# Attention with queries six tokens to a row, means in 32-column tiles, and scores on eight tiles at once

## The chip, the cores and the metric

The kernel runs on one core of a Trainium2 chip. The metric is the device time of the whole program in microseconds. One core has no second die to be compared with, so ratios are taken within one chip and one set of rounds; traces are also laid side by side across two chips (`e10` to `e13` ran on another chip than `e1` to `e9`). A span, from the first to the last instruction, is shorter than the time of the same run, in the runs below by 1.7 to 3.4 us.

In the lines of the profile PE is TensorE, DVE VectorE, ACT ScalarE, POOL GpSimd and SP SyncE. The results of PE lie in PSUM until VectorE or ScalarE copies them out; the kernel hands out PSUM's banks under the names `at`, `pk` and `pv`. A tiling says how PE's array is divided among small matmuls: `128*64` is two tiles of 128 rows by 64 columns. A filler is a matmul of zeros that only keeps PE busy.

## The reference

```python
a = exp(phi - max); a = a / sum(a)              # 8 batches, 8 heads, 576 tokens, 32 slots
k_m = einsum('bhsm,bhsd->bhmd', a, k)           # means of k and v over the tokens, d = 64
v_m = einsum('bhsm,bhsd->bhmd', a, v)
attn = softmax(q @ k_m.T / sqrt(64))            # 576 x 32 for each head
x = (attn @ v_m) ... reshape to (8, 576, 512)
x_prev = x shifted by one token
xk = mu_k * x + (1 - mu_k) * x_prev;  xr = mu_r * x + (1 - mu_r) * x_prev
out = sigmoid(xr @ w_r) * (relu(xk @ w_k)**2 @ w_v)      # 512 -> 1024 -> 512
```

The attention is small in arithmetic; the three products with the weights are large. The kernel interleaves both: the channel mix goes through the 4608 tokens in nine chunks of 512 with 16 groups of matmuls each (`pk` keys, `pr` gates, `pv` values), and the steps of one batch's attention stand between these groups at places that a table names.

## The kernel before

Tokens lie four to a row in 128 rows, with the last 64 of 576 as a fifth piece of 64 rows. The means of two heads are computed at once in 64 columns, the half of it that belongs to the other head being masked away afterwards:

```python
for j in range(NJ):                                   # NJ = 5 pieces of tokens
    for c in range(2):
        for jj in range(2):
            pr = 2 * c + jj
            nc.tensor.matmul(kvps[jj * 64:(jj + 1) * 64, c], lhsT=heads(j, pr * 64, 64),
                             rhs=kv5[:, parts, 2 * pr:2 * pr + 2, j, :], ...)
...
def tr_q(pr):                                          # queries: one head, one piece, 64 columns
    for j in range(NJ):
        for i in range(2):
            nc.tensor.matmul(ps[i * D:(i + 1) * D, j * 128:(j + 1) * 128],
                             lhsT=q5[:, 2 * pr + i, j, :], rhs=identity, is_transpose=True, ...)
...
def scores(c, hf):                                     # two tiles, one bank
    for jj in range(2):
        nc.tensor.matmul(ps[jj * 64:(jj + 1) * 64, :], lhsT=st["kmT"][:, c, jj, :],
                         rhs=st["qT"][:, 2 * c + jj, sl], ...)
...
def load_mu():                                         # mu, needed for the first two batches' mixing
    ... nc.vector.tensor_scalar_add(mu1, ps_mu, -1.0)
    for w in range(2):                                 # mu_b was loaded from ScalarE's queue at the start
        nc.vector.tensor_mul(mu_m[:, w, 0], mask, mu_b[:, w])
        nc.vector.tensor_sub(mu_m[:, w, 1], mask, mu_m[:, w, 0])
```

The softmax here doesn't subtract the row's maximum and nothing guards it: scores larger than these inputs give would overflow.

Of the kernel before, what the change touches and what calls it, by code (L numbers as in the profile page):

```python
# [17 lines left out]
STEADY = [("q2", -15), ("q0+pv", -15), ("q3+pk", -15), ("q1", -15), ("exp", -15), ("kv+pv", -14), ("z+pv",  # L18
          -14), ("nk", -13), ("nv", -13), ("load", -11), ("tk", -11), ("s3", -9), ("s1+pk", -9),
          ("s2", -8), ("s0+pv", -8), ("l0+pk", -6), ("l3", -6), ("l2", -5), ("l1+pk", -5), ("r0z",  # L20
          -4), ("r1z", -3), ("w0", -3), ("x0", 1), ("x1+pv", 2), ("w1", 2), ("x2", 7), ("x3", 8),
          ("dd", 9), ("k2d", 11), ("k0d", 13), ("r0d", 15), ("r2d", 23)]
FIRST = {
    0: [("exp", -58), ("busy23_232748", -54), ("mu", -48), ("k+pv", -47), ("z+pv", -45), ("busy1_400335",
        -45), ("q0", -43), ("nk", -41), ("busy1_690297", -41), ("q1", -39), ("tk", -39), ("s1+pv",
        -39), ("s0+pk", -38), ("q2", -37), ("busy2_979210", -37), ("l0", -36), ("q3", -32),
        ("l1+pk", -30), ("s3", -28), ("s2+pv", -26), ("r0z", -25), ("busy3_103560", -23), ("w0",
        -21), ("l2+pv", -20), ("l3+pv", -18), ("r1z", -18), ("v+pv", -15), ("busy1_899602", -15),
        ("nkx", -14), ("w1", -13), ("busy1_551200", -11), ("mk1", -11), ("mk0+pk", -11), ("mk2",
        -10), ("mk3+pv", -10), ("nrx", -5), ("load", -3), ("mr2+pv", 2), ("mr0+pk", 2), ("mr1", 2),  # L30
        ("mr3", 7)],
    1: [("exp", 5), ("k+pk", 8), ("z+pk", 8), ("nk", 9), ("tk+pk", 10), ("q3", 10), ("q2+pk", 10),
        ("q1+pv", 10), ("q0", 11), ("s0", 11), ("s2", 11), ("s3", 11), ("s1+pk", 12), ("l0", 12),
        ("l2+pv", 12), ("l1+pk", 12), ("r0z", 13), ("l3", 13), ("v", 13), ("w0", 13), ("nkx", 13),
        ("nrx", 13), ("r1z", 13), ("mk0", 13), ("w1", 13), ("mk1+pv", 13), ("mr3+pk", 14), ("mr1",
        14), ("mk3+pv", 14), ("mk2", 15), ("mr0+pv", 15), ("load", 16), ("mr2+pv", 17)],
    2: [("q3", -2), ("q0", -2), ("q1+pv", -2), ("exp", -2), ("kv", -1), ("q2", -1), ("z", -1), ("nk", -1),
        ("nv", -1), ("tk", 0), ("s2+pv", 1), ("s0", 1), ("s1", 1), ("s3", 1), ("l1", 3), ("l2+pv",
        3), ("l3", 4), ("l0", 4), ("r0z", 5), ("w0", 5), ("r1z", 5), ("x1+pv", 7), ("x0", 7), ("w1",
        7), ("load+pv", 8), ("x2", 8), ("x3+pk", 8), ("dd", 9), ("k0d", 12), ("r2d", 12), ("k2d",  # L40
        13), ("r0d", 13)],
    3: [("q0", -11), ("q2", -8), ("exp", -8), ("q1", -8), ("q3", -7), ("kv+pv", -7), ("z", -7), ("nk", -7),
        ("nv", -7), ("load+pv", -7), ("tk", -6), ("s2", -5), ("s3+pv", -5), ("s1", -5), ("s0", -5),
        ("l2+pv", -4), ("l3", -4), ("r1z", -4), ("w1", -4), ("l1", -4), ("l0+pk", -4), ("r0z", -4),
        ("w0", -2), ("x3", -1), ("x2", 1), ("x1", 7), ("x0", 8), ("dd", 8), ("k0d", 8), ("k2d", 11),
        ("r2d", 12), ("r0d", 15)],
}
ORDER = ('phi', 'k', 'q', 'wv', 'v')



NB = 4
TAIL = 512
# [3 lines left out]
def kernel(  # L57
# [24 lines left out]
    HALF = S // 2  # L82
    CT = 512
# [12 lines left out]
    qs = [const.tile([128, H, NJ, D], BF16, name=f"q{i}") for i in range(2)]  # L96
# [26 lines left out]

    def load_batch(b):
        load_phi(b, nc.gpsimd)
        load_rows(kvs[b % 2][:, 0], k[b])
        load_rows(qs[b % 2], q[b])
        load_rows(kvs[b % 2][:, 1], v[b])
# [3 lines left out]
    load_rows(qs[0], q[0], 2)  # L132
# [3 lines left out]
    for i in range(2):  # L136
        nc.vector.memset(kvs[i][64:128, :, :, NB, :].rearrange("p a h d -> p (a h) d"), 0.0)
        nc.vector.memset(ems[i][64:128, NB], 0.0)
        nc.vector.memset(qs[i][64:128, :, NB, :], 0.0)
# [5 lines left out]
    for w, mu in enumerate((moe_mu_k, moe_mu_r)):  # L145
        for jj in range(2):
            nc.scalar.dma_start(
                out=mu_b[jj * 64:(jj + 1) * 64, w],
                in_=mu.rearrange("(c j x) -> j c x", c=2, j=2)[jj:jj + 1].to_broadcast([64, 2, 2 * D]))
# [11 lines left out]
    for what in ORDER:  # L161
        if what == "wv":
            nc.gpsimd.dma_start(out=wv_sb, in_=wv_v)
        elif what == "phi":
            load_phi(1, nc.gpsimd)
        else:
            load_rows(qs[1] if what == "q" else kvs[1][:, "kv".index(what)], {"q": q, "k": k, "v": v}[what][1])
# [29 lines left out]

    def load_mu():
        ps_mu = psum.tile([128, 2 * ND], F32, name="psmu", tag="at", bufs=3)
        nc.tensor.transpose(ps_mu, mu2, ident_f)  # L200
        nc.vector.tensor_scalar_add(mu1, ps_mu, -1.0)

        for w in range(2):
            mask = maskk.rearrange("p h d -> p (h d)").unsqueeze(1).to_broadcast([128, 2, 2 * D])
            nc.vector.tensor_mul(mu_m[:, w, 0], mask, mu_b[:, w])
            nc.vector.tensor_sub(mu_m[:, w, 1], mask, mu_m[:, w, 0])


    def attention(b):
        st = {}  # L210

        def ps_tile(shape, dtype, name):

            tag = st.get("tag", "at")
            return psum.tile(shape, dtype, name=name, tag=tag, bufs={"at": 3, "pk": 2, "pv": 3}[tag])
        x0 = b * S % RING
        kv5, q5, em = kvs[b % 2], qs[b % 2], ems[b % 2]
# [9 lines left out]
        def ekv(parts):  # L227

            def go():
                w = parts.stop - parts.start  # L230
                kvps = ps_tile([128, 2, w, 2 * D], F32, "kvps")
                for i in range(w):
                    st["kv"[parts.start + i]] = kvps[:, :, i, :]
                for j in range(NJ):
                    for c in range(2):
                        for jj in range(2):
                            pr = 2 * c + jj
                            nc.tensor.matmul(kvps[jj * 64:(jj + 1) * 64, c], lhsT=heads(j, pr * 64, 64),  # L238
                                             rhs=kv5[:, parts, 2 * pr:2 * pr + 2, j, :],
                                             start=j == 0 and c == 0, stop=j == NB,  # L240
                                             skip_group_check=True)
# [11 lines left out]
        def norm_k():  # L253
            kbd = work.tile([128, 2, 2, D], BF16, name="kbd", tag="kbd")
            for c in range(2):
                nc.vector.scalar_tensor_tensor(
                    kbd[:, c].rearrange("p h d -> p (h d)"), in0=st["k"][:, c, :],
                    scalar=st["rz"][:, c:c + 1], in1=maskk.rearrange("p h d -> p (h d)"),
                    op0=AL.mult, op1=AL.mult)
            st["kbd"] = kbd  # L260

        def norm_v():
            vbd = work.tile([128, 2, 2, D], BF16, name="vbd", tag="vbd")
            for c in range(2):
                nc.vector.scalar_tensor_tensor(
                    vbd[:, c].rearrange("p h d -> p (h d)"), in0=st["v"][:, c],
                    scalar=st["rz"][:, c:c + 1], in1=maskk.rearrange("p h d -> p (h d)"),
                    op0=AL.mult, op1=AL.mult)
# [6 lines left out]
        def tr_k():  # L275
            ps = ps_tile([128, 2, 2, 64], BF16, "ktps")
            for c in range(2):
                nc.tensor.matmul(ps[:, c].rearrange("p j m -> p (j m)"),
                                 lhsT=st["kbd"][:, c].rearrange("p h d -> p (h d)"), rhs=identity,
                                 is_transpose=True, start=True, stop=True, skip_group_check=True)  # L280
            st["kmT"] = work.tile([128, 2, 2, 64], BF16, name="kmT", tag="kmT")
            nc.vector.tensor_copy(st["kmT"].rearrange("p c j m -> p (c j m)"),
                                  ps.rearrange("p c j m -> p (c j m)"))

        def tr_q(pr):
            def go():
                if "qT" not in st:
                    st["qT"] = work.tile([128, NPAIR, S], BF16, name="qT", tag="qT")
                ps = ps_tile([128, NJ * 128], BF16, "qtps")
                for j in range(NJ):  # L290
                    for i in range(2):
                        nc.tensor.matmul(ps[i * D:(i + 1) * D, j * 128:(j + 1) * 128],  # L292
                                         lhsT=q5[:, 2 * pr + i, j, :], rhs=identity,
                                         is_transpose=True, start=True, stop=True,
                                         skip_group_check=True)
                nc.vector.tensor_copy(st["qT"][:, pr, :], ps[:, 0:S])  # L296
            return go

        def scores(c, hf):
            def go():  # L300
                if "e" not in st:
                    st["e"] = work.tile([128, 2, S], BF16, name="e", tag="e")
                ps = ps_tile([128, HALF], F32, "scps")
                sl = slice(hf * HALF, (hf + 1) * HALF)
                for jj in range(2):
                    nc.tensor.matmul(ps[jj * 64:(jj + 1) * 64, :], lhsT=st["kmT"][:, c, jj, :],  # L306
                                     rhs=st["qT"][:, 2 * c + jj, sl], start=True, stop=True,
                                     skip_group_check=True)
# [256 lines left out]
```

## Time and profile before

| | before |
|---|---|
| time, median of 3 (range) | 233.19 us (232.72 to 234.55) |
| span of the profiled run | 231.6 us |
| first wide matmul (`pk`) | 23.25 us |
| from there to the start of PE's last instruction | 202.8 us |
| PE after that instruction's start to the end | 5.6 us |
| length of a chunk in the steady state | 22.7 us |

The span falls into a start, in which PE waits for loads and for a chain of small steps; a middle, in which the load queue is full as well as PE; and a steady state from about 100 us on, in which PE alone is full. A chunk's length is taken between the starts of the first ReLU activations of two chunks, as the trace records them: where PE is the bound, what a change saves must show there, chunk by chunk.

The profile page of the kernel before, the packets (count, megabytes, mean rate, sizes) and the load queue (packets, megabytes, share of 16 DMA engines):

```profile
DMA packets 49365, 31.49 MB, mean 136 GB/s; under 512 B 14920, under 2 KB 43856, under 8 KB 49344
q0 software_dynamic: 41520, 20.91, 64.9%
```

### The profile page before, as it was taken

How to read it: one execution, taken by the hardware profiler on the slowest of the kernel's cores; microseconds unless marked ns; L12 is line 12 of the kernel's file. 1: busy time of each engine (PE TensorE's matmuls, PEld its weight loads, DVE VectorE, ACT ScalarE, POOL GpSimd, SP SyncE). 2: the span in 40 equal slices, each digit the busy share in tenths (PEclk: the TensorE clock that was granted, in tenths of full speed). 3: DMA queues.
4: the chain of work that ended last, by engine and by line, in shares of the span. 5: the costliest groups of instructions: out<-in, count | busy, mean ns of one | idle time of the engine just before them, and what ended most of it. 6: DMA issues, size and time to landing. Idle time of an engine off the chain costs nothing.

```text
span 231.6 us, 4343 instructions
## 1 busy us (share of the span) xinstructions
PE 217.9 (94%) x1649; PEld 108.4 (47%) x1649; DVE 142.6 (62%) x353; ACT 161.2 (70%) x305; POOL 54.1 (23%) x74
## 2 busy tenths in 40 slices
PE   7688999789999999999999999999999999999990
PEld 3344444355435455445444774464444444444450
DVE  3436744396467896588638966896687767425222
ACT  3116688852986894998599859976988865765860
POOL 8573451553455508101900000000000000000000
PEclk9958999999999999999999999999999999999998
DMA  6999999999999999992899300420023043023033
GB/s 134 190 197 213 224 200 224 196 237 245 213 226 193 255 207 261 189 220 96 159 178 165 91 3 0 93 91 0 3 92 91 1 93 91 0 92 91 3 91 91
DMA packets 49365, 31.49 MB, mean 136 GB/s; under 512 B 14920, under 2 KB 43856, under 8 KB 49344
## 3 DMA queue, kind: packets, MB, share of 16 engines
q0 software_dynamic: 41520, 20.91, 64.9%
q1 hardware_dynamic: 7008, 9.77, 14.5%
q10 hardware_dynamic: 816, 0.52, 0.9%
q8 instruction: 13, 0.21, 0.4%
q14 instruction: 8, 0.07, 0.1%
HBM read 38.54 MB, written 9.44 MB: 207 GB/s over the span
## 4 chain that ended last, share of the span: by engine, by line
PE 78%; DMA 10%; ACT 5%; DVE 3%; issue 1%; POOL 1%; DVEq 0%; POOLq 0%
PE pk L480 25%; PE pv L513 24%; PE pr L494 13%; DMA q<-in_q_dram 10%; PE qtps L292 4%; PE kvps L238 3%; PE nops L346 2%; PE scps L306 2%; PE zps L319 1%; ACT sg L501 1%; ACT sg L502 1%; DVE atn L333 1%; ACT sg L499 1%; PE zps L248 1%; ACT e L309 1%
## 5 line engine op out<-in xcount | busy, mean ns | idle before, releaser
L480 PE MATMUL pk<-xkT,wk 128*128 128x512 bf16 (+1 forms) x320 | 67.2, 358 | 0.2 <-ACT xrT L409 0.2
L513 PE MATMUL pv<-wv,sq 128*128 128x512 bf16 (+1 forms) x296 | 66.2, 373 | 0.0
L484 ACT ACTIVATE rl<-pk 128x512 bf16<-128x512 f32 x72 | 42.8, 598 | 29.6 <-PE pk L480 29.6
L485 DVE TENSOR_TENSOR sq<-rl 128x512 bf16<-128x512 bf16 x72 | 29.8, 424 | 28.0 <-ACT rl L484 27.6
L515 DVE TENSOR_TENSOR o<-sg,pv 128x512 f32<-128x512 f32 (+1 forms) x37 | 23.9, 672 | 32.5 <-ACT sg L502 25.2
L513 PEld LDWEIGHTS <-sq 128*128 128x128 bf16 x296 | 28.6, 98 | 32.3 <-issue 0.7
L480 PEld LDWEIGHTS <-wk 128*128 128x128 bf16 x320 | 29.9, 98 | 28.1 <-issue 0.8
L494 PE MATMUL pr<-wr,xrT 128*128 128x512 bf16 x144 | 35.5, 380 | 0.0
L499 ACT ACTIVATE sg<-pr 128x512 f32<-128x512 f32 x36 | 22.0, 614 | 8.9 <-PE pr L494 8.9
L494 PEld LDWEIGHTS <-xrT 128*128 128x128 bf16 x144 | 12.8, 98 | 15.1 <-issue 2.3
L501 ACT ACTIVATE sg<-sg 128x1024 f32<-128x1024 f32 x18 | 19.0, 1057 | 0.6
L502 ACT ACTIVATE sg<-sg 128x1024 f32<-128x1024 f32 x18 | 19.0, 1057 | 0.6
L309 ACT ACTIVATE e<-scps 128x288 bf16<-128x288 f32 x32 | 11.6, 445 | 9.8 <-PE scps L306 9.7
L296 DVE COPY qT<-qtps 128x576 bf16<-128x576 bf16 x32 | 13.1, 452 | 6.8 <-PE qtps L292 6.6
L350 ACT CAST x<-nops 128x288 bf16<-128x288 f32 x48 | 16.8, 423 | 0.0
L371 DVE TENSOR_SCALAR mu_d<-diff,mu 128x576 bf16<-128x576 bf16 x48 | 15.5, 364 | 0.0
L292 PE MATMUL qtps<-identity,q 128*64 128x128 bf16 x320 | 13.4, 233 | 1.5 <-DMA q<-in_q_dram 1.4
L321 ACT ACTIVATE lz<-zps 128x288 f32<-128x288 f32 x32 | 11.4, 410 | 3.2 <-PE zps L319 3.2
L292 PEld LDWEIGHTS <-q 128*64 128x64 bf16 x320 | 10.6, 116 | 5.8 <-DMA q<-in_q_dram 2.6
L333 DVE TENSOR_TENSOR atn<-e,lz 128x576 bf16<-128x576 bf16 x16 | 12.0, 752 | 2.0 <-ACT lz L326 1.8
L107 POOL DMA_DIRECT2D phm<-in_phi_dram x7 | 6.3, 896 | 27.4 <-ACT em L222 24.4
L238 PE MATMUL kvps<-kv,em 128*64 128x256 bf16 (+1 forms) x200 | 10.8, 254 | 1.6 <-DMA kv<-in_k_dram 1.6
(67 smaller groups left out, 211.8 us busy)
## 6 DMA issues: line engine op xcount, KB each, us to landing
out_dram<-o SPq DMA_DIRECT2D x37, 128.0 KB, 2.4
kv<-in_k_dram POOLq DMA_DIRECT2D x8, 512.0 KB, 11.3
out_dram<-o SPq DMA_DIRECT2D x16, 256.0 KB, 2.7
phm<-in_phi_dram POOLq DMA_DIRECT2D x7, 512.0 KB, 11.9
q<-in_q_dram POOLq DMA_DIRECT2D x7, 512.0 KB, 12.2
kv<-in_v_dram POOLq DMA_DIRECT2D x7, 512.0 KB, 12.5
wk<-in_moe_w_k_dram POOLq DMA_DIRECT2D x2, 512.0 KB, 10.0
wv<-in_moe_w_v_dram POOLq DMA_DIRECT2D x1, 1024.0 KB, 15.6
```

What stands on the lines that cost most here:

```text
L238: nc.tensor.matmul(kvps[jj * 64:(jj + 1) * 64, c], lhsT=heads(j, pr * 64, 64), rhs=kv5[:, parts, 2 * pr:2 * pr + 2, j, :], start=j == 0 an ...
L292: nc.tensor.matmul(ps[i * D:(i + 1) * D, j * 128:(j + 1) * 128], lhsT=q5[:, 2 * pr + i, j, :], rhs=identity, is_transpose=True, start=True ...
L350: nc.scalar.copy(st["x"][:, 2 * c + jj, sl], pss[jj])
L480: nc.tensor.matmul(pk[:, lo:hi], lhsT=wk_sb[:, di, fi * 128:(fi + 1) * 128], rhs=xk_T[:, di, c0:c0 + hi - lo], start=(di == 0), stop=(di = ...
L484: nc.scalar.activation(rl, pk, AF.Relu)
L485: nc.vector.tensor_mul(st["sq"][:, fi, :], rl, rl)
L494: nc.tensor.matmul(pr, lhsT=xr_T[:, di, c0:c0 + 128], rhs=wr_sb[:, di, :], start=(di == 0), stop=(di == ND - 1))
L499: nc.scalar.activation(sg[:, ts % 2], pr, AF.Exp, scale=-1.0)
L501: nc.scalar.activation(sg, sg, AF.Ln, bias=1.0)
L502: nc.scalar.activation(sg, sg, AF.Exp, scale=-1.0)
L513: nc.tensor.matmul(pv[:, cols], lhsT=st["sq"][:, fi, ts * 128:(ts + 1) * 128], rhs=wv_sb[:, fi, cols], start=(fi == 0), stop=(fi == NF - 1))
L515: nc.vector.tensor_mul(o[:, cols], st[ts // 2][:, ts % 2, cols], pv[:, cols])
```

## The change

Its intent is to give TensorE less to do for the attention. Queries are loaded six tokens to a row in 96 rows, so a transpose takes two tokens of one head at full width, and the tail piece is gone; even tokens come before odd ones in a batch. The means take 32 columns for each head, four tiles at once, and nothing masked is computed. The scores take two row tiles (even and odd tokens) by four column tiles, eight at once, in two banks. All steps were given new places and new banks, and mu's broadcast is loaded later, by SyncE's queue. Besides, batches 0 and 1 take their reciprocals in halves, and 32 fillers become 18. The lines below are shortened.

```diff
-    for c in range(2):
-        for jj in range(2):
-            pr = 2 * c + jj
-            matmul(kvps[jj * 64:(jj + 1) * 64, c], lhsT=heads(j, pr * 64, 64),
-                   rhs=kv5[:, parts, 2 * pr:2 * pr + 2, j, :])
+    for h in range(H):
+        c, g = divmod(h, 4)
+        matmul(kvps[g * M:(g + 1) * M, c], lhsT=em[:, j, h, :], rhs=kv5[:, parts, h, j, :])
...
-    for j in range(NJ):
-        for i in range(2):
-            matmul(ps[i * D:(i + 1) * D, j * 128:(j + 1) * 128], lhsT=q5[:, 2 * pr + i, j, :], rhs=identity)
+    for i in range(2):
+        for j in range(NQ // 2):
+            matmul(ps[:, i, j], lhsT=qs[b % 2][:, 2 * pr + i, 2 * j:2 * j + 2, :], rhs=identity[:QR, :QR])
...
-    for jj in range(2):
-        matmul(ps[jj * 64:(jj + 1) * 64, :], lhsT=kmT[:, c, jj, :], rhs=qT[:, 2 * c + jj, sl])
+    for g in range(4):
+        for hf in range(2):
+            matmul(pss[hf][m, :], lhsT=kmT[r, c, m], rhs=qT[r, 4 * c + g])
...
+def load_mu_b():                       # step "mub": a memset of one column, then the broadcast loads
+    nc.vector.memset(mu_b[:, :, 0, 0:1], 0.0)
+    ... nc.sync.dma_start(out=mu_b[...], in_=mu...)
+def spread_mu():                       # step "mum": what stood at the end of load_mu
-STEADY = [("q2", -15), ("q0+pv", -15), ...     # places and banks of the steps (cut)
+STEADY = [("exp", -20), ("q3", -16), ...
```

## The prediction

> **What bounds the kernel now.** I read the page first: the slices, then the groups by line and form, then the waits of TensorE, then single stretches of the timeline.
>
> ```profile
> PE 217.9 (94%) x1649; PEld 108.4 (47%) x1649; DVE 142.6 (62%) x353; ACT 161.2 (70%) x305; POOL 54.1 (23%) x74
> ...
> PE   7688999789999999999999999999999999999990
> ...
> PEclk9958999999999999999999999999999999999998
> DMA  6999999999999999992899300420023043023033
> ```
>
> A slice is 5.8 us. From the fifth slice on TensorE is full; before it there are holes, and two slices (5 and 8 tenths) at a lowered clock. DMA is full for the first 100 us or so. So there are three stages: a start of 23 us (the first big matmul begins at 23.25 us), a middle to about 72 us in which DMA is full too, and a rest of 155 us in which PE alone is full. The waits of PE confirm it: the table, of which the five largest lines stand below (us in total, times, longest), sums to 8.1 us over the whole run, all of it before some 72 us.
>
> ```profile
> PE kvps L238 <- DMA kv<-in_k_dram: 1.6, 1, 1.6
> PE qtps L292 <- DMA q<-in_q_dram: 1.4, 3, 0.5
> PE idle L195 <- DVE zeros L135: 1.2, 1, 1.2
> PE mxps L400 <- DVE vm L381: 0.9, 1, 0.9
> PE scps L306 <- DVE qT L296: 0.6, 1, 0.6
> ```
>
> A full PE says nothing of how well it is used, so I looked at how far apart the starts are. The timeline of PE at 106 us and at 70 us:
>
> ```profile
> 106.33 0.38 PE L480 MATMUL pk<-xkT,wk 128*128 128x512 bf16 x1
> 106.64 0.29 PE L346 MATMUL nops<-atn,vbd 64*128 64x288 bf16 x2
> 106.87 1.31 PE L292 MATMUL qtps<-identity,q 128*64 128x128 bf16 x40
> 108.11 1.04 PE L480 MATMUL pk<-xkT,wk 128*128 128x512 bf16 x4
> ```
>
> ```profile
> 70.58 1.28 PE L238 MATMUL kvps<-kv,em 128*64 128x256 bf16 x20
> 71.80 0.40 PE L248 MATMUL zps<-ones,em 128*128 128x1 bf16 x10
> 72.06 1.89 PE L513 MATMUL pv<-wv,sq 128*128 128x512 bf16 x8
> 73.79 0.27 PE L278 MATMUL ktps<-identity,kbd 128*128 128x128 bf16 x2
> ```
>
> Four prices come out of the starts. (a) Eight 512-wide matmuls from 72.06 to 73.79: 216 ns each, that is 512/2.4 GHz + 2.5 ns; I use N/2.4 + 2.5 for other widths. (b) Two tiles of 64 columns run side by side: 40 transposes from 106.87 to 108.11 are 1.24 us, 20 pairs of 56 ns (the price of one 128-wide matmul) and 0.12 for the changes of tiling. The means by construction (233 ns for such a transpose) are no cost. (c) A change of tiling costs about 0.1 us: from the lone 512-wide matmul to the 64-row pair there are 0.31 us, of which 0.216 are its own; from that pair to the 64-column tiles 0.23, of which 0.122 are its own. (d) Ten full-width loads with a one-column matmul take 0.26 us, so a load and a matmul need no more than 26 ns.
>
> **What the Trainium skill says.** "TensorEngine Tiling (Array Packing)", Key Properties, says that changing the tiling mode drains TensorE; the trace agrees and prices it at some 96 ns each way. "TensorE: Matmul & The Clock Gate", Part 3 (The mechanism), says that matmuls on different 32-wide strips run concurrently, with some 4 ns between starts; the trace shows it for two tiles (b), not yet for four or eight. "TensorEngine Tiling (Array Packing)", Restrictions, says that column tiling disables Fast Weight Load. The trace fits weakly: loads of 64 columns have a mean of 109 to 116 ns, those of 128 columns 98, and behind 56 ns pairs neither shows. "DMA: Bandwidth & Descriptors", Specifications, puts the size for line rate at 512 B; here 14920 packets are below that, and the 64-row rest of q supplies 512 of them a batch.
>
> **The change, part by part**, in PE time between starts. The counts are from the order of the instructions of the two kernels.
>
> Queries: 320 half-width transposes, 160 pairs x 56 ns = 9.0 us, become 192 full-width ones of 96 rows. They carry the full 128x128 tiling, so they need no drain, and cost 96/2.4 + 2.5 = 42.5 ns: 8.2 us. Gain 0.8 us.
>
> Means (k_m, v_m): 80 matmuls of 128 wide and 120 of 256 wide, in pairs: 40 x 56 + 60 x 109 = 8.8 us. After: 160 of 64 wide and 240 of 128 wide, in fours of 32 columns: 40 x 29 + 60 x 56 = 4.5 us. The half that the mask threw away is no longer computed. Gain 4.2 us, if four tiles overlap as two do.
>
> Scores: 64 matmuls of 288, 32 pairs x 122.5 = 3.9 us; after it 128 in 16 groups of eight (2 row x 4 column tiles), each 122.5 and seven starts of some 3 ns: 2.3 us. Gain 1.6 us.
>
> Changes of tiling: 109 before, 85 after, since the queries no longer need any and the score and value groups lie closer together: 24 x 0.096 = 2.3 us.
>
> The mixed outputs of batches 0 and 1 lose 16 short matmuls in pairs: about 0.1 us. The 680 wide matmuls, the denominators, the values and the sums are the same. Fillers: 32 become 18, 3.0 us of PE; but they stand in the start, in waits, and I count nothing for them.
>
> Sum: 0.8 + 4.2 + 1.6 + 2.3 + 0.1 = 9.0 us. Walking both orders with these prices gives that 7.7 us of it lies after the first wide matmul and 1.3 before. The same walk on the kernel before meets its trace to within 1 us from 72 us to the end, so there a saved us of PE is a saved us of time, as long as nobody else becomes the bound: ACT is 16 of 20 us busy there, DVE 14.5.
>
> Start. Here PE waits (for k until 10.1 us, for q until 12.05, then for a chain of transposes, copies, exponentials, logarithms). The change takes 256 KB of broadcast mu out of the way of phi and k, halves q's packets (1536 to 768 a batch, now of 1.5 KB read), and splits the reciprocals of batch 0 in halves: each step of that chain after the logarithm takes some 0.4 us instead of 0.68 to 0.75. Against it: only 5 fillers stand before the first k matmul where 23 stood, so PE may run the chain at half clock, but the chain hardly consists of PE work. I estimate 1.5 us earlier.
>
> Middle. DMA is full, and q's waits at 51 and 63.5 us show that it paces PE. The packets of the load queue take 64.9% of 16 x 231.6 us over 41520, 58 ns each. Per batch 768 fewer of these, but with the same bytes; about a third of that product, 1 us a batch (an estimate), is what DMA should gain, about what PE gains (1.1 to 1.3 us a batch). So I let the middle have its PE gain.
>
> DVE and ACT: almost the same instructions, 8 splits more on each in the start; kbd without the mask; differences in three pieces (1152, 768 and 380) in place of 1536, 508 and 256, the same total. No load there.
>
> Total: 233.2 - 7.7 - 1.5 + 0.8 for waits that a denser schedule meets = 224.8 us.
>
> **Rivals.**
> 1. Small tiles bound by issue, not by streaming. If a load and a matmul cost the 26 ns of (d) each time, the means cost 400 x 26 = 10.4 us, more than before, the scores 3.3 us. The gain shrinks from 9.0 to about 2.1 us: some 231 us. For it: no run yet has more than two tiles at once. Against: in pairs two loads and two matmuls pass in 53 to 56 ns, and even there the starts inside a pair are a few ns apart, so issue is not at its limit; the queue fills during the wide matmuls ahead.
> 2. The middle stays paced by DMA or by the chain of vectors and activations, and PE only waits more. Then only what lies after 72 us counts, four batches at 1.1 to 1.3, about 4.8 us, and the start: about 228 us. For it: the full DMA row, waits on vm, atn and qT. Against: in the walk above PE waits for only some 7 us in the whole middle, and DMA gets lighter too.
> 3. Queries of 96 rows count as another tiling and drain. Then some 3 blocks a batch at 0.2 us: 4.8 us back, about 229. For it: nothing but the odd row count. Against: the instructions carry the full tiling.
> 4. Banks: the scores take two banks at once and steps share banks with the gates and keys; with ACT at 80% a late eviction would stall PE. 1 to 3 us worse. The steps have been given new banks and places throughout, which speaks for a schedule made to fit.
>
> **Range and chances.** Everything as worked out and a good start: 222. Rivals 2 or 4 in part: 226 to 228. Rival 1 or 3 in full: 229 to 231. I give 1 and 3 one chance in ten together, 2 some one in seven. 80% range 221.5 to 228.3; the limit for faster is 228.5, so faster 0.89, within 2% 0.09, slower 0.02.
>
> **What would show it.** The means: 20 matmuls' stretch of 1.22 us from start to start becomes 40 in about 0.7 (ten fours at 56 ns, and a drain); near 1.1 would be rival 1. Scores of one batch: 16 in about 0.4 us with the drain. Queries: 24 at 42 to 43 ns with no gap of 0.1 before or after; a gap would be rival 3. Packets under 512 B fall from 14920 to about 10800. The first wide matmul starts near 21.7 us instead of 23.25; waits of PE stay few after 72 us. The prediction is wrong if PE shows idle stretches after 72 us, or if the wide matmuls no longer lie 216 ns apart.

## More of the kernel before

The timeline of PE in the start (start us, length us, engine and line, operation, tiling and shape, count, idle before it and what ended that):

```profile
10.11 0.87 PE L238 MATMUL kvps<-kv,em 128*64 128x128 bf16 x20 [1.60 <-DMA kv<-in_k_dram]
...
14.77 0.69 PE L306 MATMUL scps<-qT,kmT 128*64 128x288 bf16 x4 [0.43 <-DVE kmT L282]
```

k's means begin as soon as k lands at 10.11 us, the first scores follow 4.7 us later.

## The result

The changed kernel gives the right result. It took 224.92 us (median of 4, 224.43 to 225.48) where the kernel before took 233.1 us in the same rounds. The ratio is 0.9639, with a 95% interval of 0.959 to 0.9688. Executions over 1.5% slower than the fastest of the same kernel are left out of the means. Ratios here are the mean time of one kernel's runs over the mean of the other's runs of the same rounds, so not quite the ratio of the medians quoted.

| from the traces, us | before | after | difference |
|---|---|---|---|
| first wide matmul | 23.25 | 24.86 | +1.61 |
| from it to PE's last start | 202.78 | 193.05 | -9.73 |
| of that, PE's work by the prediction's prices (estimate) | 195.3 | 187.6 | -7.7 |
| of that, the rest (waits and gaps) | 7.5 | 5.5 | -2.0 |
| after PE's last start | 5.59 | 5.24 | -0.35 |
| span | 231.62 | 223.16 | -8.46 |

The work is an estimate: every matmul and every change of tiling after the first wide matmul (92 changes before, 72 after) at the prediction's prices. Summed again it came to 195.1 and 187.2, so the split is good to some 0.4 us. The price N/2.4 + 2.5 rests on two spacings of the trace, 216 ns for 512 columns and 56 for 128: 160 ns for 384 columns. The total is as predicted; two of its terms are not. The page of the kernel after, the same rows as in the prediction, and the packets:

```profile
PE   4359999899999998999999999999999999999991
...
PEclk9999999999999999999999999999999999999999
DMA  6999999999999999999993300330132033033033
...
DMA packets 43349, 31.49 MB, mean 141 GB/s; under 512 B 10952, under 2 KB 37840, under 8 KB 43328
```

The first two slices of PE hold 4 and 3 tenths where they held 7 and 6: most fillers are gone. From the fourth slice on PE is as full as before. The clock row is full from its first slice, which should not be believed for the start: twelve transposes took 1.17 us there (at 11.29 us, starts 80 ns apart) and take 0.68 us later (starts 42 ns apart), so the clock was low. The clock's first record in this trace comes only at 21.3 us. Packets under 512 B went to 10952, where the prediction had some 10800, with the bytes unchanged.

The timeline of PE in the steady state answers to that of the two stretches in the prediction:

```profile
124.02 0.42 PE L325 MATMUL qtps<-identity,q 96*128 96x96 bf16 x6
124.27 1.04 PE L518 MATMUL pk<-xkT,wk 128*128 128x256 bf16 x8
...
125.47 0.74 PE L264 MATMUL kvps<-kv,em 128*32 128x128 bf16 x40
126.14 1.92 PE L518 MATMUL pk<-xkT,wk 128*128 128x256 bf16 x16
...
133.20 0.44 PE L341 MATMUL scps<-qT,kmT 64*32 64x288 bf16 x16
133.57 1.04 PE L532 MATMUL pr<-wr,xrT 128*128 128x512 bf16 x4
```

Read the starts, not the lengths. Forty means take 0.67 us until the next group starts, that is ten fours at 56 ns and 0.1 us for the change of tiling. Sixteen scores take 0.37 us: two groups of 122.5 ns and 0.1 us. Six transposes of 96 rows take 0.25 us, 42 ns each, and nothing is added before the full-width matmul that follows, though the tiling is printed as `96*128`. A chunk lasts 21.56 and 21.50 us there, where it lasted 22.75 and 22.70: 1.2 us less, and the prices had said 1.15.

The start went the other way. The timeline of PE, and then that of VectorE, of the kernel after; last, VectorE's second reading of the broadcast in the kernel before:

```profile
9.22 0.72 PE L264 MATMUL kvps<-kv,em 128*32 128x64 bf16 x40 [1.12 <-DMA kv<-in_k_dram]
...
16.04 0.79 PE L341 MATMUL scps<-qT,kmT 64*32 64x288 bf16 x8 [1.84 <-DVE qT L328]
```

```profile
13.23 0.43 DVE L230 TENSOR_TENSOR mu_m<-maskk,mu_b 128x256 f32<-128x256 bf16 x1 [2.08 <-DMA mu_b<-in_moe_mu_k_dram]
...
14.54 0.42 DVE L230 TENSOR_TENSOR mu_m<-maskk,mu_b 128x256 f32<-128x256 bf16 x1 [0.42 <-DMA mu_b<-in_moe_mu_r_dram]
...
15.34 0.28 DVE L308 COPY kmT<-ktps 128x256 bf16<-128x256 bf16 x1
15.54 1.54 DVE L328 COPY qT<-qtps 128x576 bf16<-128x576 bf16 x4
```

```profile
10.41 0.43 DVE L205 TENSOR_TENSOR mu_m<-maskk,mu_b 128x256 f32<-128x256 bf16 x1 [0.85 <-DMA mu_b<-in_moe_mu_r_dram]
```

k is 0.9 us earlier in this profile, but the first scores are 1.3 us later, 6.8 us after k instead of 4.7. Scores need `kmT` and `qT`, which VectorE copies out of PSUM; and VectorE, which took its work in the order of the program, stood before that at the spreading of mu, 2.08 and 0.42 us long, because mu's broadcast is now loaded late. Before the change that broadcast had landed by 10.4 us.

The waits of PE from 23 us on, of the kernel after (us in total, times, longest us; two lines of 0.2 us are left out):

```profile
PE zps L355 <- ACT e L345: 0.8, 2, 0.5
PE scps L341 <- DVE kmT L308: 0.6, 1, 0.6
PE mxps L439 <- DVE o L553: 0.5, 2, 0.3
PE nops L382 <- DVE atn L369: 0.3, 1, 0.3
```

The whole list sums to 2.6 us where that of the kernel before sums to 3.8; gone are the waits for q (0.9 us after the first wide matmul) and those for `vm` (1.1 us). No wait for a load is left. Two waits are for a bank that has still to be read: `mxps` for VectorE's `o` (0.5 us) and `nops` for ScalarE's `rl` (0.2 us, in a line left out). Three waits, 1.0 us in all, come after 72 us, at 84.9, 88.0 and 89.7 us, which the prediction had named as a sign of being wrong; after 92 us there are none.

### The profile page after: what moved, and what is told of

It is laid out like the page before. It is cut to its first block, busy times and chain, and to the rows that moved or that the text cites. A ratio compares the mean times of both kernels' runs of the same rounds, so it can differ in the third digit from the quotient of the medians.

```text
span 223.2 us, 4576 instructions
## 1 busy us (share of the span) xinstructions
PE 205.6 (92%) x1755; PEld 101.5 (45%) x1755; DVE 142.3 (64%) x356; ACT 159.9 (72%) x309; POOL 47.7 (21%) x66
## 2 busy tenths in 40 slices
DMA packets 43349, 31.49 MB, mean 141 GB/s; under 512 B 10952, under 2 KB 37840, under 8 KB 43328
## 4 chain that ended last, share of the span: by engine, by line
PE 80%; ACT 6%; DVE 5%; DMA 3%; POOL 1%; issue 1%; SPq 1%; DVEq 0%; POOLq 0%
PE pk L518 28%; PE pv L551 25%; PE pr L532 13%; DMA mu_b<-in_moe_mu_r_dram 3%; PE qtps L325 2%; PE kvps L264 2%; PE nops L382 2%; PE zps L355 2%; PE idle L209 2%; PE scps L341 1%; DVE atn L369 1%; PE mxps L439 1%; DVE o L553 1%; ACT e L345 1%; PE zps L274 1%
## 5 line engine op out<-in xcount | busy, mean ns | idle before, releaser
L518 PE MATMUL pk<-xkT,wk 128*128 128x512 bf16 (+1 forms) x320 | 69.4, 358 | 0.0
L518 PEld LDWEIGHTS <-wk 128*128 128x128 bf16 x320 | 29.0, 98 | 26.2 <-issue 1.6
L345 ACT ACTIVATE e<-scps 128x288 bf16<-128x288 f32 x32 | 10.8, 430 | 10.1 <-PE scps L341 10.1
L407 DVE TENSOR_SCALAR mu_d<-diff,mu 128x576 bf16<-128x576 bf16 x48 | 16.3, 383 | 0.2
L386 ACT CAST x<-nops 128x288 bf16<-128x288 f32 x48 | 16.0, 417 | 0.0
L369 DVE TENSOR_TENSOR atn<-e,lz 128x576 bf16<-128x576 bf16 (+1 forms) x20 | 12.3, 632 | 2.9 <-ACT lz L362 2.5
L325 PE MATMUL qtps<-identity,q 96*128 96x96 bf16 x192 | 12.4, 215 | 0.6 <-DMA q<-in_q_dram 0.6
L325 PEld LDWEIGHTS <-q 96*128 96x128 bf16 x192 | 11.0, 103 | 3.9 <-DMA q<-in_q_dram 0.8
L362 ACT ACTIVATE lz<-lz 128x576 f32<-128x576 f32 (+1 forms) x20 | 11.4, 596 | 0.0
L248 ACT ACTIVATE em<-phm 128x1024 bf16<-128x1024 f32 x8 | 8.4, 1055 | 3.2 <-DMA phm<-in_phi_dram 3.2
```

The costliest lines, as they stand in the source:

```text
L325: nc.tensor.matmul(ps[:, i, j], rhs=identity[:QR, :QR], is_transpose=True, lhsT=qs[b % 2][:, 2 * pr + i, 2 * j:2 * j + 2, :].rearrange("p ...
L386: nc.scalar.copy(st["x"][:, 2 * c + jj, sl], pss[jj])
L407: nc.vector.tensor_scalar_mul(t[:, i], st["d"][:, pr + i, :], mu1[:, o:o + 1])
L518: nc.tensor.matmul(pk[:, lo:hi], lhsT=wk_sb[:, di, fi * 128:(fi + 1) * 128], rhs=xk_T[:, di, c0:c0 + hi - lo], start=(di == 0), stop=(di = ...
```

## The experiments

Theory: in the steady state the prices of starts hold, each by itself; the start is late because mu's broadcast blocks VectorE; and the middle still has a limit in the load queue, which was hidden because the start was late. Rivals: the start is late because of the low clock; the middle is free because q's packets are fewer; the schedule as a whole, and not the small tiles, brought the gain.

### Does the price of the small tiles hold by itself?

`e4_pairs` is the changed kernel with the means in 64 columns again. Its output is wrong, which doesn't matter for the time.

```diff
-    for h in range(H):
-        c, g = divmod(h, 4)
-        matmul(kvps[g * M:(g + 1) * M, c], lhsT=em[:, j, h, :], rhs=kv5[:, parts, h, j, :])
+    for pr in range(H // 2):
+        c, jj = divmod(pr, 2)
+        matmul(kvps[jj * 64:(jj + 1) * 64, c], lhsT=heads(j, pr * 64, 64), rhs=kv5[:, parts, 2 * pr:2 * pr + 2, j, :])
```

> The changed kernel with the means computed in pairs of 64-column tiles with both heads as moving data, as before, and nothing else changed: half of the heads' columns is then dropped, so the result is wrong on purpose; vectors, activations and order are the same. Theory (four 32-column tiles run side by side and the means are worth their PE time): 3.7 us more PE time after the first wide matmul (60 pairs at 109 instead of 60 fours at 56 ns, and batch 1's 20 pairs at 56 instead of fours at 29), so about 228.6 us. Rival (the gain of the change is its new schedule, the tiles only fill slack): within 1 us of 224.9.

Measured: 228.64 us (228.57 to 229.31), ratio to before 0.979 [0.9747, 0.9832]. The profile's timeline of PE in the steady state:

```profile
127.95 1.28 PE L264 MATMUL kvps<-kv,em 128*64 128x256 bf16 x20
129.17 1.92 PE L518 MATMUL pk<-xkT,wk 128*128 128x256 bf16 x16
```

Those means last 1.22 us again instead of 0.67. The chunks of the steady state are 0.54 us longer, priced at 0.53. So four tiles at once are worth 3.7 us of the change by the medians of the times and 3.5 by the traces (first wide matmul to PE's last start), priced at 3.7.

`e5_before_fours` does that part alone in the kernel before.

> The kernel before with the means alone changed to 32-column tiles (masked afterwards from the 64 wide result), old queries, scores, order and schedule; the result is right. Theory: 3.5 us less PE time after the first wide matmul, all of it in the time where PE is full (2.7 of it after 72 us), so 229.6 to 230.5 us instead of 233.1. Rival (the old schedule's middle is paced by DMA and by the vector chain): only what lies after 72 us counts and waits grow in the middle, 230.5 to 231.5.

Measured: 230.68 us (230.43 to 230.83), ratio 0.987 [0.9828, 0.9911]; the start of the last chunk moved from 209.92 to 206.98 us. The time is 0.2 us over the theory's end and so just inside the rival's range. What was lost can be named, in two places. In the first chunk 0.44 us of the priced 0.95 came through; a wait for `vm` grew there from the 0.9 us shown in the prediction:

```profile
PE mxps L404 <- DVE vm L383: 1.2, 1, 1.2
```

And a steady chunk gained 0.41 us instead of 0.53, with no wait: the forty means have the same starts as in the changed kernel, but the sums that follow them here start 0.24 us after the last mean's own price, where every other change of tiling takes 0.10.

### Does each change of tiling cost what was priced?

`e6_apart` moves one step of the scores and one of the values in the steady state by one place, so that each stands alone between wide matmuls.

```diff
-("s1+aa", -8)    ("x1+aa", 6)
+("s1+aa", -9)    ("x1+aa", 7)
```

> The changed kernel with one score step and one value step of the six steady blocks moved by one wide group, so that steps which stood side by side stand apart: 97 changes of tiling instead of 85, the same matmuls. Theory (each change costs 96 ns of PE time, and PE is full there): 12 x 0.096 = 1.2 us more, about 226.1 us; in the trace the wide groups after 100 us come 0.2 to 0.4 us a chunk later. Rival (changes of tiling hide behind the queue): within 0.3 us of 224.9.

Measured: 229.6 us (229.25 to 231.41), ratio 0.9846 [0.9781, 0.9911], 4.7 us slower than the changed kernel and far outside what was expected. The timeline of PE says why:

```profile
134.38 0.30 PE L382 MATMUL nops<-atn,vbd 64*128 64x288 bf16 x2
134.60 0.29 PE L341 MATMUL scps<-qT,kmT 64*32 64x288 bf16 x1
135.42 0.31 PE L341 MATMUL scps<-qT,kmT 64*32 64x288 bf16 x7 [0.52 <-ACT x L386]
```

The values and the scores now follow each other and use the same banks. The first of eight scores starts at once, the other seven 0.82 us later, when ScalarE has copied the values out of PSUM. In the changed kernel the eight start within 24 ns. From the values to the first `pv` of the chunk there are 4.58 us here and 3.48 in the changed kernel; 0.8 of those 1.10 us are this wait, and 0.3 are left for three more changes of tiling. That fits the price but is a remainder. The starts give the price directly: from 105 us on, in the kernels before and after and here, each change of tiling whose records are complete adds 89 to 105 ns to the price of the matmul ahead of it. What the run does show is the prediction's fourth rival: "TensorEngine Tiling (Array Packing)", PSUM Bottleneck, warns that the copy out of PSUM can become the bottleneck once tiles are faster. In the schedule as given such waits sum to 0.7 us, all before 92 us; one place further they cost 0.8 us a batch.

### What made the start late?

`e1_mum_late` moves the spreading of mu behind the copies of q; loads stay as they are.

```diff
-("busy1_9643", -46), ("mum", -43), ... ("q2+v", -35), ("s0+av", -33),
+("busy1_9643", -46), ... ("q2+v", -35), ("mum", -35), ("s0+av", -33),
```

> The changed kernel, with the four vector steps that spread mu put behind the copies of the keys and queries of batch 0 in VectorE's order (they stood ahead of them, and waited for the mu loads until 13.2 and 14.5 us while the keys had been ready at 11.5 us). Theory: in the changed kernel VectorE, in order, held the start back behind the late mu; then the first scores start near 14.3 us instead of 16.04, the first wide matmul near 23.2 instead of 24.87, and the time is 1.2 to 1.8 us less than the changed kernel's 224.9 (about 223.4). Rival: the start is paced by the half clock of PE or by v and wk; then the first wide matmul stays within 0.4 us of 24.87 and the time within 0.4 us of 224.9.

Measured: 225.19 us (224.44 to 227.06), ratio 0.965 [0.9579, 0.972]. The timeline of PE in that run:

```profile
14.07 0.44 PE L341 MATMUL scps<-qT,kmT 64*32 64x288 bf16 x8
...
22.91 2.75 PE L518 MATMUL pk<-xkT,wk 128*128 128x512 bf16 x11
...
53.54 0.75 PE L264 MATMUL kvps<-kv,em 128*32 128x128 bf16 x40 [1.09 <-DMA kv<-in_v_dram]
```

The start is 1.96 us earlier, as the theory said. Other runs share these starts: with mu spread ahead of the copies the first wide matmul came at 24.86, 24.91, 25.10 and 25.56 us (the changed kernel, `e4`, `e6`, `e12`), with mu behind them at 22.91, 23.93 and 22.83 (`e1`, `e9`, `e10`). The two groups stand apart, by 1.9 us in the mean: the block on VectorE is shown. The time is not lower, and the third line names what took it back: v of batch 2 is now waited for, 1.09 us. The first two chunks lead the changed kernel by 1.96 and 1.97 us, all later ones by 0.80.

`e2_fillers` tests the rival: 25 fillers up front instead of 5, so that the clock is high in the start (`busy2` to `busy22`).

> The changed kernel with 25 filler matmuls instead of 5 ahead of the first k matmul, nothing else. Theory: the start is held by VectorE behind mu, so a warm clock changes little: transposes of q at 42 ns instead of 80 and fillers at 216 instead of 427 ns, but the first wide matmul comes only 0 to 0.5 us earlier. Rival (half clock is what cost the predicted gain of the start): it comes 1.5 us or more earlier, time 223.4 or less.

Measured: 224.66 us (224.52 to 225.71), ratio 0.9623 [0.9578, 0.9668]; first wide matmul at 24.09 us, 0.78 earlier. That lies between both expectations, and the changed kernel itself, run again (`e12_after` below), had its first wide matmul at 25.56 us, 0.70 later than in its first profile. Nor did the fillers keep the clock up: the trace records half the clock from 13.33 to 20.15 us, and of the two groups of q transposes only the first has starts 42 ns apart, the second 80. So the rival is only half tested and what the clock is worth in the start is not settled. `e1_mum_late` won its 1.96 us without those fillers.

`e8_mu_early` loads mu's broadcast from ScalarE's queue at the start, as before the change.

```diff
-("mub", -55),
+for w, mu in enumerate((moe_mu_k, moe_mu_r)): ... nc.scalar.dma_start(out=mu_b[...], in_=mu...)
```

> The changed kernel with the broadcast mu loaded from ACT at the very start, as before the change. Theory: k lands some 0.8 us later (about 10 instead of 9.2 us), but VectorE no longer waits for mu in front of the copies, so the first wide matmul comes at 23.5 to 24.2 instead of 24.87; the end moves by less than that, as v of batch 2 still paces PE at about 54 us: 224.2 to 225. Rival (moving mu late was worth it): first wide matmul later than 25 us, and the time above 225.3.

Measured: 224.79 us (224.64 to 225.09), ratio 0.962 [0.958, 0.9661]. First wide matmul at 22.93 us, as early as with the late spreading and earlier than the 23.5 to 24.2 expected; k's means began at 9.96 us instead of 9.22, but in five traces with the changed kernel's start they begin anywhere from 9.22 to 10.27, so that k comes earlier with mu late is not shown. Again the lead was lost: PE waits 1.70 us for v of batch 2 at 54.2 us, and the last chunk leads by 0.08 us.

### What takes the start back?

`e7_q_halves` undoes the lighter packets alone: q in two loads of three tokens a row.

```diff
+for a in range(2):
+    nc.gpsimd.dma_start(out=dst[:, :, a], in_=src[:, :, a])     # three tokens of a row each
```

> The changed kernel with q loaded in two halves of three tokens to a row (768 B read, 384 B written): 1536 packets a batch as before the change instead of 768, the same bytes, places and matmuls. Theory (until 54 us PE is held to the pace of DMA, and the lighter q load is part of why the middle has few waits): DMA time of q grows by 0.8 to 1.2 us a batch, v of batch 2 lands 2 to 3 us later, PE waits for it near 53 us, and the time grows by 1.5 to 3 us (226.4 to 228). Rival (the new schedule alone removed the waits): under 0.5 us.

Measured: 225.55 us (225.15 to 226.2), ratio 0.9654 [0.9609, 0.9698]. The load queue of the changed kernel, then of this run (packets, megabytes, share of the engines' span):

```profile
q0 software_dynamic: 35248, 20.91, 63.1%
```

```profile
q0 software_dynamic: 41536, 20.91, 66.9%
```

That is 8.6 us more, 1.07 us a batch, just what the prediction estimated. But PE waits for nothing that it did not wait for without them; all nine chunks are 0.22 to 0.23 us later, the difference of the start. The median is 0.63 us above the changed kernel's, about as far as two medians of the changed kernel lie apart (224.92 and 225.51). So the lighter packets are real and bring no time here: at the pace and start of the changed kernel, loads come just soon enough anyway.

`e9_v_first` puts v ahead of q in the loads of batch 2, and that batch's query steps later, on top of `e1_mum_late`.

```diff
-2: ("phi", "k", "q", "v")    2: [... ("q0", -1), ("q1+v", -1), ("q3+a", 0), ... ("s0+kv", 2) ...
+2: ("phi", "k", "v", "q")    2: [... ("q0", 2), ("q1+v", 2), ("q3+a", 2), ... ("s0+kv", 3) ...
```

> The kernel with mu spread late (first wide matmul at 22.9 us, of whose 1.95 us gain 1.1 us was lost waiting for v of batch 2 at 53.5 us), with v of batch 2 loaded ahead of its q, and the query steps of batch 2 two to three wide groups later. Theory: the wait for v at 53.5 us goes, q is used when it has landed, and 0.7 to 1.1 us of the start's gain reaches the end: the activations of the last chunk start near 200.0 us against 201.0 and 201.8; time 223.0 to 223.9. Rival (any order only moves the wait, as all that is loaded by 54 us is needed): the wait for q takes the place of that for v, 224.5 or more.

Measured: 224.19 us (223.51 to 224.71), ratio 0.9591 [0.9547, 0.9636]. The wait for v is gone. The first wide matmul came at 23.93 us, the second chunk leads by 1.07 us, but the third by only 0.27, and the time lies between theory and rival: moving the steps of the queries brought waits for `qT` (0.4 us) and `xkT` (0.2 us) and less room. An order of loads shifts the shortage; it does not remove it.

`e10_no_q2` removes it: `e1_mum_late` without the load of q for batch 2, so that batch computes with older queries. It is wrong, though the comparison with the reference did not notice: the softmax over such small scores hardly depends on q, I suppose. It was run on another chip.

> Wrong on purpose: the late spread of mu once more, and the load of q for batch 2 (read after v's place in the queue is taken) left out, so that v of batch 2 stands third instead of fourth in its loads. Theory: the 1.96 us that the late spread wins at the start is paid back at some 53 us because the load queue, full since the start, delivers v of batch 2 no earlier (a wait of 1.1 us there, lead 0.80 us from the third chunk on). With 590 KB of reads less ahead of it that wait is gone (under 0.2 us), the lead is still 1.8 to 2.1 us in the last chunk (its first activation at 199.7 to 200.0 us against 201.80), and the time is 222.7 to 223.7 us. Rival: v is late for another reason (its buffer comes free late, or it is issued late): the wait stays over 0.8 us, the lead in the last chunk under 1.1 us, the time 224.2 us or more.

Measured: 223.23 us (222.69 to 225.22), ratio 0.9574 [0.952, 0.9627]. First wide matmul at 22.83 us, no wait for v, and the lead is 2.04 to 2.05 us from the first chunk to the last (which starts at 199.75 us instead of 201.80). It is 2.3 us faster than the changed kernel on the same chip (`e12_after`, 225.51 us). With q's 590 KB (as written) out of the queue ahead of v, a start that is 2 us shorter is worth 2 us. The theory met every number; the rival that v's buffer comes free late fell. That v is issued late did not fall with it: v's two loads were issued at 33.3 and 38.8 us instead of 38.4 and 40.6 and had landed by 49.8 us instead of 54.0, so whether q's bytes or its place among the issues counts is not separated.

The traces add one thing that no run tests. With an early start v did not land when it had landed before, but later: its first load at 53.5, 54.1 and 54.2 us in `e1_mum_late`, `e8_mu_early` and `e13_both` (below), against 52.1 to 52.8 in the changed kernel and in `e4`, `e6`, `e7` and `e12`. Between 50 and 52 us the stores of the first outputs, which an earlier start brings forward, moved 0.28 to 0.33 MB in those three runs and at most 0.01 MB in the five, and the load queue 0.31 to 0.35 MB instead of 0.52 to 0.56. Stores ahead of v are thus a likely part of the wait.

The last three runs shared rounds. They were run on another chip. `e12_after` is the changed kernel once more, `e13_both` joins the late spreading of mu to the fillers, and `e11_six` is a candidate: that start, and k, v and phi read six tokens to a row of 96 like the queries.

```diff
-kvs = [const.tile([128, 2, H, NJ, D], BF16) ...]     for j in range(NJ):     # e11_six: 5 pieces
+kvs = [const.tile([QR, 2, H, NQ, D], BF16) ...]      for j in range(NQ):     # 6 pieces of 96 rows
```

> The changed kernel unchanged, for a close comparison in the same rounds: 224.4 to 225.5 us; its first wide matmul between 24.5 and 25.2 us, showing how much the start differs from run to run.

> The late spread and the 25 fillers together, loads as in the changed kernel. Theory (the load queue takes the start back): first wide matmul near 22.2 us, but v of batch 2 is waited for 1.3 to 2 us near 53 us and the last chunk starts 0.4 to 0.9 us earlier than in the changed kernel: 224.0 to 224.6 us. Rival (no giving back): 222.2 to 222.9 us.

> A candidate: the start with the late spread and 25 fillers, and k, v and phi read six tokens to a row of 96 as the queries are, which makes the loads lighter (768 packets instead of 1536 for k and for v of a batch) but the means 48 products for v and k instead of 40, and the sums 12 instead of 10. Priced: 12 fours at 56 ns instead of 10, and 2 sums at 26 ns, 0.16 us a batch, 1.3 us in all. Theory (the load queue takes the start back): the lead of the start, some 2.0 to 2.7 us, is kept, no wait for v of batch 2, so 224.9 - 2.4 + 1.3 = 223.8 us, 223.0 to 224.4; packets under 512 B below 6000. Rival (the lead is lost to the chain of vectors and activations whatever the loads do): 225.3 us or more. If 96 rows with tiles of 32 columns drain against the other tiling, two drains a batch more or less show, 1 us.

| | time, us (median of 6) | ratio to before | first wide matmul | wait for v of batch 2 | last chunk |
|---|---|---|---|---|---|
| `e12_after` | 225.51 (224.94 to 226.52) | 0.9652 [0.9611, 0.9692] | 25.56 | none | 202.48 |
| `e13_both` | 224.95 (223.9 to 227.23) | 0.964 [0.9593, 0.9688] | 22.53 | 2.6 | 204.09 |
| `e11_six` | 225.18 (224.69 to 225.5) | 0.9641 [0.9604, 0.9677] | 23.57 | none | 201.75 |

`e12_after` missed its range for the first wide matmul by 0.36 us: the start of one and the same kernel differs by at least 0.7 us from one execution to another, which bounds what single profiles say of it. In `e13_both` the earliest start meets the longest wait, as the theory had it, though its median of 224.95 us is above the range. Its profile caught its slowest run (227.23 us, granted clock 0.973): after the wait the clock is recorded at half from 56.2 to 59.6 us, so its times after the wait are not used. In that profile the wait reads:

```profile
54.24 0.63 PE L264 MATMUL kvps<-kv,em 128*32 128x128 bf16 x32 [1.91 <-DMA kv<-in_v_dram]
```

`e11_six` has 29798 packets instead of 43349, 1864 of them under 512 B, and no wait for a load. Its steady chunks last 21.61 to 21.66 us, 0.11 us more than the changed kernel's, near the 0.16 priced for two more fours and sums. But its first wide matmul was only 1.3 us ahead of the changed kernel's first profile, its first chunk 0.4 us longer (a wait of 0.3 us for the activated phi stands in it), and in the last chunk 0.05 us of the lead are left. Its time missed the theory's range and comes close to the rival's limit. I cannot say from one profile how much of the miss is chance of the start. None of the correct versions is shown to beat the changed kernel: their intervals all overlap its own.

## Why the prediction was right, and where not

- **PE's work: right.** The term of 7.7 us after the first wide matmul was met: steady chunks are 1.2 us shorter where 1.15 was priced. Means, scores and queries each have the spacing that was said; the means' share is isolated by `e4_pairs` (3.7 us). Taken alone, in `e5_before_fours`, they gave 2.6 us of time, the rest going into a longer wait in the first chunk and a dearer change of tiling. The prediction's counts and sums hold when redone; one reading does not: PE alone is not full from 72 us on, as DMA is full to some 104 us.
- **Changes of tiling: right.** Starts show 0.09 to 0.10 us for each, in the kernel after as before; only `e5_before_fours` has one of 0.24. The run meant to isolate it met a wait for banks besides, and leaves 0.3 us for three, as a remainder.
- **The start: wrong.** The step that failed is "I estimate 1.5 us earlier". The start came 1.6 us later, an error of 3.1 us. I had counted mu's broadcast only as 256 KB out of the way of phi and k, and had not asked who waits for the broadcast: VectorE does, in order, ahead of the copies that the first scores need. `e1_mum_late` and `e8_mu_early` take that away in two ways and both win 1.9 to 2.0 us of start.
- **The waits: wrong in the other direction.** "0.8 for waits that a denser schedule meets" was 2.0 us less instead, an error of 2.8. Gone are the waits for q and `vm`; which of the new places did that no run isolates. Part of it goes with the late start: `e1_mum_late`, `e8_mu_early` and `e13_both` show that an earlier start brings 1.1 to 2.6 us of waiting back at v of batch 2. I had added the two as if they were independent, and they are not while loads are awaited up to some 54 us. So two errors of some 3 us pull to opposite sides. That they left the sum right by 0.1 us is luck: `e1_mum_late` pays back only 1.1 of its 1.96 us, and `e12_after`, starting 0.7 us later still, took the same 193.0 us after its first wide matmul.
- **"The middle keeps its PE gain since DMA gets lighter": the outcome right, the reason not.** The estimate of 1 us a batch was good (1.07 in `e7_q_halves`), but without it PE did not wait either.
- **The rivals.** One and three did not occur: issue is not the limit at four and eight tiles, and 96 rows do not drain. Two, the middle paced by the loads, is not seen in the changed kernel and stands right behind it. Four, banks, shows with 0.7 us in the schedule as given, less than the 1 to 3 us feared, and costs some 0.8 us a batch one place further.

## What to carry to other kernels

Price small matmuls by the distance of starts and the changes of tiling between them, and the part of a span where PE alone is full can be forecast to a tenth of a microsecond a chunk. For a start, ask of every load that is moved not only what it makes room for but which in-order engine will stand waiting for it, and what stands behind that. And do not add gains of two stages in a row when a queue runs through both: an earlier start only moved the wait to v of batch 2, until a load of 590 KB ahead of it was left out.

## What the Trainium skill lacked or had wrong

- "TensorEngine Tiling (Array Packing)", Key Properties, says that a change of mode drains, without a price. The runs show 0.09 to 0.10 us for each change, and 0.24 us for one kind, from fours of 32 columns to one-column sums in `e5_before_fours`.
- "TensorEngine Tiling (Array Packing)", Tiling Modes, lists tiles of 128, 64 and 32 rows and does not say what an operand of 96 rows counts as. Here 96 x 96 transposes took 42 ns each, and going to and from full-width matmuls cost nothing; means of 96 rows in 32 columns passed too (`e11_six`).
- "TensorE: Matmul & The Clock Gate", Part 4 (PE-mode transpose), gives some 275 ns for a transpose in the context of a kernel, and no distance between starts. The profile's length is 0.2 us here as well, but starts are 42 ns apart, and that is what counts.
- No page says that the clock row of a profile can be full before the clock's first record; the caveat on the clock's trace events in "TensorE: Matmul & The Clock Gate", Part 1, would be the place. Here it was full while twelve transposes took 1.17 us, against 0.68 later.
